# Strassen's seven products for y·w1 and y·w2, and an earlier hand-over of attention's memory

## The chip, the cores and the metric

The kernel runs on one core of a Trainium2 chip. The metric is the device time of one execution, in microseconds (us). Engines are named as in the profile: PE multiplies matrices, PEld loads its weights, DVE, ACT and POOL work on elements, SP issues the DMA transfers.

## The reference

Attention's output becomes the tokens of a first MLP, and its output those of a second, gated one. All of it is float64 on the host's side for the weights and float32 in the results:

```python
x = attention(q, k, v)                      # 4 x 576 tokens, 512 wide
h = x @ w_in; x = np.maximum(0.01*h, h) @ w_out     # 512 -> 2048 -> 512
a = x @ w1; b = x @ w2                      # 512 -> 1024 each
out = ((a * b) @ w3) @ w_out2               # 1024 -> 1024 -> 512
```

There are 2304 tokens. The kernel gets the weights as 64-bit words and converts them on the chip.

## The kernel before, in words

**Arithmetic.** Each float32 operand is kept as two parts, hi and lo; `split` makes hi with a copy (L107) and lo with a subtraction (L108). `mm3` (L112 to L114) then needs three matmuls for one product.

**Stages.** Attention (32 rounds) is interleaved with the first MLP. The MLP runs in 8 chunks of 320 or 256 tokens, with 16 turns f in each: `hidden(c, f)` is 12 matmuls into `ps_h`, `project(c, f)` 12 matmuls into `ps_x`, two turns later. Between them ACT makes `g`, and `gs` is split from it by DVE and POOL. A running number `turn` counts all turns, 16 to a chunk; at turn 80 chunk 5 begins, at 112 chunk 7.

**The fold.** w3·w_out2 is one 1024 x 512 matrix `wp`. Its 24 conversions (`conv3`: 8 pieces of w_out2, then 16 of w3) go through a class `Convert`: SP loads 512 KB of 64-bit words into one of two `rawf` buffers, POOL scales them into `wf` (L103), ACT makes two halves `rf` (L143, L145), DVE shifts and adds (L146, L147). The pieces of w_out2 are split and written to DRAM (`wo_dram` in the profile, tiles `wo2_` in the program's order). A piece of w3 is transposed by PE (`ps_w3T`, L546) and split into `w3T`. After nine conversions `wp_step` runs: 6 matmuls of 512 columns with a `wo2` tile read back from DRAM. The fold needs the memory that attention used, so it starts with chunk 5 (`C_LATE`).

**w1 and w2.** In chunk 7 their 16 pieces are converted (`raww`, `wr`) and stay in SBUF as `w12`.

**The gate and the final product.** For each of 6 chunks of 384 tokens and each of 8 column blocks i, `gate` runs 24 matmuls of 384 columns (`ps_ab`) for y·w1 and y·w2; ACT copies one half (`a`), DVE multiplies it by the other (`ab`), and `p` is split from that by ACT and POOL. `final` multiplies `p` by `wp` (`ps_y`, 512 columns, 24 matmuls for each of 18 blocks of 128 tokens).

The order of instructions on PE, DVE, ACT and POOL is set when the program is built, by a scheduler that reorders them within their dependences; each engine then runs its list strictly in order. SP's list is the queue of all DMA issues.

## Time and profile before

| | |
|---|---|
| median of 3 runs | 917.64 us (916.98 to 919.58) |
| the profiled execution | 918.02 us, span in the trace 916.2 us |
| PE busy | 880.8 us, 96% of the span |
| DVE, ACT, POOL busy | 345.9, 354.5, 247.8 us |
| DMA | 95.94 MB, mean 105 GB/s |

The span runs from the first instruction to the last; the execution is 1.8 us longer. PE's busy time counts overlapping matmuls once. In the trace of this kernel most matmuls of one L112-to-L114 group start evenly, so the distance between starts, not the mean duration, is the time that one takes.

### The profile page before, as it was taken

The page shows a single profiled execution, that of the slowest core. Times are in us where ns is not written, and L with a number is a line of the kernel's source. Part 1 is how long each engine was busy: PE and PEld are TensorE (multiplying, and loading weights), DVE is VectorE, ACT ScalarE, POOL GpSimd, SP SyncE. Part 2 cuts the span into 40 slices and gives each one's busy share as a digit, 9 for nine tenths or more (in the row PEclk, how much of TensorE's full clock was granted, in tenths as well). Part 3 has the DMA queues.
Part 4 walks back from the last instruction along what each step waited for, and adds up shares of the span by engine and source line. Part 5 has one row for each costly group of instructions (what it writes and reads, how often), then busy time and mean ns, then how long its engine had stood idle before and what let it go on. Part 6 is the DMA issues. An engine that isn't in the chain of part 4 may idle for free.

```text
span 916.2 us, 16026 instructions
## 1 busy us (share of the span) xinstructions
PE 880.8 (96%) x6456; PEld 832.4 (91%) x6456; DVE 345.9 (38%) x699; ACT 354.5 (39%) x904; POOL 247.8 (27%) x288
## 2 busy tenths in 40 slices
...
GB/s 170 313 271 129 180 19 57 83 48 73 49 44 78 45 14 62 47 252 282 235 293 271 211 201 160 202 79 1 46 24 35 35 35 24 12 24 12 12 24 35
DMA packets 110938, 95.94 MB, mean 105 GB/s; under 512 B 69520, under 2 KB 94352, under 8 KB 110864
## 3 DMA queue, kind: packets, MB, share of 16 engines
...
q8 instruction: 51, 0.84, 0.4%
...
## 4 chain that ended last, share of the span: by engine, by line
PE 82%; DVE 6%; ACT 3%; DMA 3%; SPq 2%; issue 2%; POOL 1%; DVEq 0%; POOLq 0%; ACTq 0%
PE ps_ab L112 7%; PE ps_ab L114 7%; PE ps_ab L113 7%; PE ps_h L113 6%; PE ps_h L114 6%; PE ps_x L112 6%; PE ps_h L112 6%; PE ps_x L114 6%; PE ps_x L113 6%; PE ps_y L113 4%; PE ps_y L112 4%; PE ps_y L114 4%; PE ps_s L328 2%; PE ps_o L389 2%; PE ps_wp L114 2%
## 5 line engine op out<-in xcount | busy, mean ns | idle before, releaser
L112 PE MATMUL ps_h<-x,win 128*128 128x320 f32 (+1 forms) x512 | 154.7, 303 | 3.6 <-DMA v<-in_v_dram 2.3
L113 PE MATMUL ps_h<-x,win 128*128 128x320 f32 (+1 forms) x512 | 155.4, 304 | 1.1 <-DVE x L422 1.1
L113 PE MATMUL ps_x<-gs,wout 128*128 128x320 f32 (+1 forms) x512 | 152.8, 299 | 2.4 <-DVE gs L108 2.4
L114 PE MATMUL ps_h<-x,win 128*128 128x320 f32 (+1 forms) x512 | 154.4, 302 | 0.0
L112 PE MATMUL ps_x<-gs,wout 128*128 128x320 f32 (+1 forms) x512 | 152.1, 299 | 1.1 <-DVE x L509 1.1
L114 PE MATMUL ps_x<-gs,wout 128*128 128x320 f32 (+1 forms) x512 | 152.7, 299 | 0.0
L112 PE MATMUL ps_ab<-ys,w 128*128 128x384 f32 x384 | 130.1, 339 | 0.0
L114 PE MATMUL ps_ab<-ys,w 128*128 128x384 f32 x384 | 130.0, 339 | 0.0
L113 PE MATMUL ps_ab<-ys,w 128*128 128x384 f32 x384 | 130.0, 338 | 0.0
L616 DVE TENSOR_TENSOR ab<-a,ps_ab 128x384 f32<-128x384 f32 x48 | 26.6, 554 | 253.0 <-ACT a L614 247.9
L107 DVE CAST gs<-g 128x320 fp32r<-128x320 f32 (+1 forms) x128 | 49.7, 391 | 153.6 <-ACT g L473 153.4
L108 POOL TENSOR_TENSOR p<-ab,p 128x384 fp32r<-128x384 f32 x48 | 48.5, 1011 | 218.6 <-ACT p L107 218.6
L108 POOL TENSOR_TENSOR gs<-g,gs 128x320 fp32r<-128x320 f32 (+1 forms) x80 | 66.4, 831 | 145.2 <-DVE gs L107 145.2
L112 PEld LDWEIGHTS ps_h<-x,win 128*128 128x128 f32 x512 | 97.9, 192 | 5.3 <-ACT x L420 4.2
L113 PEld LDWEIGHTS ps_x<-gs,wout 128*128 128x128 f32 x512 | 96.9, 189 | 3.8 <-DVE gs L108 2.9
L113 PEld LDWEIGHTS ps_h<-x,win 128*128 128x128 f32 x512 | 98.3, 192 | 2.1 <-DVE x L422 1.3
L112 PEld LDWEIGHTS ps_x<-gs,wout 128*128 128x128 f32 x512 | 96.5, 189 | 2.6 <-DVE x L509 1.3
L114 PEld LDWEIGHTS ps_h<-x,win 128*128 128x128 f32 x512 | 98.4, 192 | 0.3
L114 PEld LDWEIGHTS ps_x<-gs,wout 128*128 128x128 f32 x512 | 96.9, 189 | 0.5
L473 ACT ACTIVATE g<-ps_h 128x320 f32<-128x320 f32 (+1 forms) x128 | 51.4, 403 | 115.2 <-PE ps_h L114 114.1
L614 ACT COPY a<-ps_ab 128x384 f32<-128x384 f32 x48 | 23.0, 480 | 143.9 <-PE ps_ab L114 143.9
L112 PEld LDWEIGHTS ps_ab<-ys,w 128*128 128x128 f32 x384 | 72.0, 188 | 1.2
...
## 6 DMA issues: line engine op xcount, KB each, us to landing
...
```

Source lines behind the costliest of these rows:

```text
L107: copy_on(e_hi)(hi, src)
L108: e_lo.tensor_tensor(lo, src, hi.bitcast(F32), op=ALU.subtract)
L112: nc.tensor.matmul(ps, a[1], b[0], start=first, stop=False)
L113: nc.tensor.matmul(ps, a[0], b[1], start=False, stop=False)
L114: nc.tensor.matmul(ps, a[0], b[0], start=False, stop=last)
L328: nc.tensor.matmul(ps[j * QB : (j + 1) * QB, i - bl.start], qt[d, i * QB : (i + 1) * QB], kt[d, first_key(i, plain) : first_key(i, plain) ...
L389: nc.tensor.matmul(ps[j * D : (j + 1) * D, i * QB : (i + 1) * QB], vt[i][:, h + j, :], t[:, i, j * QB : (j + 1) * QB], start=True, stop=True,)
L473: nc.scalar.activation(g, ps, AF.Prelu, alpha=SLOPE)
L614: nc.scalar.copy(t, ps[0][:, :TB])
L616: nc.vector.tensor_tensor(g, t, ps[1][:, :TB], op=ALU.mult)
```

## The change

The second MLP's y·w1 and y·w2 are computed together as one 2 x 2 block product: tokens in two halves, the inner dimension in two halves, and [w1 w2] as two column blocks. Seven products (S1 to S7) take the place of eight, each 6 matmuls of 384 columns. A chunk now has 768 tokens, and there are 3 (`NCB`). The weight sums are made once, while converting (`keep_w12`, `wsum`), split and written to DRAM (`wq_dram`, 56 blocks of 256 KB); 28 tiles of two blocks are read back by `load_wq` into the 16 slots of the first MLP's `win`. Twelve of them stay; the other 16 are loaded for each chunk of tokens into slots that earlier tiles gave up. `split_y` makes seven sums of y, and `gate` recombines the seven PSUM results.

Attention's memory is given up at turn 72 (chunk 4, f = 8) in place of turn 80. The fold runs from there in 16 turns, one or two steps in a turn, and the conversion of w1 and w2 from turn 88 (chunk 5, f = 8) to the end of chunk 6. In chunk 7 the tiles of `wq` are loaded as the `win` slots come free. The final products of a chunk follow its gates.

```diff
-    NCB = T // TB
+    NCB = T // TB // 2
...
+    NS = 7
+    S1, S3, S4, S7, S6, S5, S2 = range(NS)
+    H2 = NC // 2
+    wq_dram = tc.dram_tile([P, NI * NS, 2 * H2 * P], F32, name="wq_dram")
+    yf, ys, pr, wq, w_f32 = {}, {}, {}, {}, {}
+
+    def keep_w12(m, i):
+        def finish(w, e_hi, e_lo):
+            w_f32[m] = w.rearrange("p (h c) -> p h c", h=2)
+            if m == 0:
+                return
+            a, b = w_f32.pop(0), w_f32.pop(1)
+            t, t_b = (
+                late.tile([P, n, 2, H2 * P], F32R, tag=f"wq{n}", name=f"wq{i}_{n}", bufs=m)
+                for n, m in ((S7, 1), (NS - S7, 1))
+            )
+            sums = (
+                (S1, a[:, 0], b[:, 1], ALU.add), (S7, a[:, 1], b[:, 1], ALU.subtract),
+                (S6, b[:, 0], a[:, 0], ALU.subtract), (S5, a[:, 0], a[:, 1], ALU.add),
+                (S2, b[:, 0], b[:, 1], ALU.add),
+            )
+            u = late.tile([P, len(sums), H2 * P], F32, tag="wsum", name=f"wsum{i}", bufs=1)
+            for j, (_, x, y, op) in enumerate(sums):
+                (nc.gpsimd if j % 2 else nc.vector).tensor_tensor(u[:, j], x, y, op=op)
+            split(t[:, S3, 0], t[:, S3, 1], a[:, 0], nc.scalar, nc.vector)
+            split(t[:, S4, 0], t[:, S4, 1], b[:, 1], nc.scalar, nc.vector)
+
+            split(t[:, S1, 0], t[:, S1, 1], u[:, 0], nc.scalar, nc.gpsimd)
+            nc.sync.dma_start(wq_dram[:, i * NS : i * NS + S7, :], t.bitcast(F32))
+            split(t_b[:, :, 0], t_b[:, :, 1], u[:, 1:], nc.scalar, nc.vector)
+            nc.sync.dma_start(wq_dram[:, i * NS + S7 : (i + 1) * NS, :], t_b.bitcast(F32))
+
+        return finish
+
+    def load_wq(j):
+
+        t = win_p.tile([P, 2, 2, H2, P], F32R, tag="win", name=f"wq{len(wq)}_{j}", bufs=NF)
+        nc.sync.dma_start(t.bitcast(F32), wq_dram[:, 2 * j : 2 * j + 2, :])
+        for x in range(2):
+            wq[divmod(2 * j + x, NS)] = t[:, x]
...
+    NWQ = NI * NS // 2
+    NWQ_STAY = 12
...
+        ops = {
+            S1: ((0, 0), (1, 1), ALU.add), S3: ((0, 1), (1, 1), ALU.subtract),
+            S4: ((1, 0), (0, 0), ALU.subtract), S7: ((1, 0), (1, 1), ALU.add),
+            S6: ((0, 0), (0, 1), ALU.add),
+        }
+        if m in ops:
+            (h0, x0), (h1, x1), op = ops[m]
+            u = yp.tile([P, TB], F32, tag="ysum", name=f"ysum{c}_{cc}_{m}", bufs=2)
+            (nc.gpsimd if m % 2 else nc.vector).tensor_tensor(u, t[:, h0, x0], t[:, h1, x1], op=op)
+        else:
+            u = t[:, 1, 1] if m == S5 else t[:, 0, 0]
+        split(y[:, 0, cc], y[:, 1, cc], u, nc.scalar, nc.vector if m % 2 else nc.gpsimd)
...
+        ps = {}
+
+        def product(m, out):
+            ps[m] = out
+            w, y = wq[i, m], ys[c, m]
+            for k in range(H2):
+                mm3(out, parts(w, k), parts(y, k), k == 0, k == H2 - 1)
+
+        def kept(m, nm):
+            t = fin.tile([P, TB], F32, tag=nm, name=f"{nm}{c}_{i}", bufs=2)
+            nc.scalar.copy(t, ps[m])
+            return t
+
+        both = [bank2(f"ps_ab{c}_{i}_{x}") for x in range(2)]
+        product(S1, both[0][:, 0, :TB])
+        product(S3, both[0][:, 1, :TB])
+        t1, t3 = kept(S1, "s1"), kept(S3, "s3")
+        product(S4, both[1][:, 0, :TB])
+        t4 = kept(S4, "s4")
+        product(S7, both[1][:, 1, :TB])
+        a1 = fin.tile([P, TB], F32, tag="a1", name=f"a1_{c}_{i}", bufs=2)
+        nc.vector.tensor_tensor(a1, t1, ps[S7], op=ALU.add)
+        nc.gpsimd.tensor_tensor(a1, a1, t4, op=ALU.add)
+        product(S6, side_bank(f"ps_ab{c}_{i}_6")[:, :TB])
+        nc.vector.tensor_tensor(t1, t1, ps[S6], op=ALU.add)
+        nc.gpsimd.tensor_tensor(t1, t1, t3, op=ALU.add)
+        product(S5, side_bank(f"ps_ab{c}_{i}_5")[:, :TB])
+        nc.vector.tensor_tensor(a1, a1, ps[S5], op=ALU.subtract)
+        nc.vector.tensor_tensor(t3, t3, ps[S5], op=ALU.add)
+        product(S2, bank(f"ps_ab{c}_{i}_2")[:, :TB])
+        nc.vector.tensor_tensor(t4, t4, ps[S2], op=ALU.add)
+        nc.vector.tensor_tensor(t1, t1, ps[S2], op=ALU.subtract)
+
+        for x, (a, b) in enumerate(((a1, t4), (t3, t1))):
+            nc.vector.tensor_tensor(a, a, b, op=ALU.mult)
+            gg = fin.tile([P, 2, TB], F32R, tag="p", name=f"p{c}_{x}_{i}", bufs=2 * NI)
+            split(gg[:, 0], gg[:, 1], a, nc.scalar, nc.gpsimd)
+            pr[2 * c + x, i] = gg
...
-        C_LATE = 5
+        T_FOLD, T_GATE = 72, 88
+        WQ_LAG = 3
...
+                conv.rest()
+                late_es.close()
+                xsA_es.close()
+                y_es, yp = pool("y", "right")
+                load_y(0, 0)
...
+                if turn == T_FOLD:
+                    step(*[stream] * 200)
+                    att_es.close()
...
+                if turn == T_GATE:
+                    while conv3.made < len(conv3.jobs) or conv3.done or w3T:
+                        fold_step()
+                    fold_es.close()
+                    late_es, late = pool("late", "right")
...
+                        jobs, late_tile("raw", U64, 2), late_tile("w", I32, 3), late_tile("r", I32, 2),
...
-                if c < C_LATE:
+                if turn < T_FOLD:
                     pace(c)
+                elif turn < T_GATE:
+                    fold_step()
+                    if f % 2:
+                        fold_step()
                 elif c < NCH - 1:
-                    fold_step()
+                    if f % 8 != 7:
+                        conv.step()
                 lagged()
                 if c == NCH - 1:
-                    conv.step()
-                    if 2 <= f < 2 + NI:
-                        load_wp(f - 2)
-                    if 3 <= f < 3 + NI:
-                        split_wp(f - 3)
-                    if 11 <= f < 11 + NC:
-                        split_y(0, f - 11)
-                    if f == 11 + NC - 1:
-                        load_y(1)
+                    if f >= WQ_LAG:
+                        load_wq(f - WQ_LAG)
+                    if f < H2 * NS:
+                        split_y(0, f // NS, f % NS)
+                    if f == NS - 1:
+                        load_y(0, 1)
+        for j in range(NF - WQ_LAG, NF):
+            load_wq(j)
         while todo:
             project(*todo.pop(0))
-        conv.step()
 
         xsB_es.close()
         wo2_es.close()
+        mlp_es.close()
         fin_es, fin = pool("fin", "left")
         for c in range(NCB):
+            if c > 0:
+                for j in range(NWQ_STAY, NF):
+                    load_wq(j)
             for i in range(NI):
                 gate(c, i)
-                if c > 0 and 1 <= i < 1 + TB // P:
-                    final(c - 1, i - 1)
-                if i >= NI - NC and c + 1 < NCB:
-                    split_y(c + 1, i - (NI - NC))
-            if c + 2 < NCB:
-                load_y(c + 2)
-        for tb in range(TB // P):
-            final(NCB - 1, tb, 2 if tb == TB // P - 1 else 1)
-        for es in (fin_es, late_es, mlp_es, wo_es, win_es, xsA_es):
+                if c == 0:
+                    load_wp(i)
+                    split_wp(i)
+                for j in range(NF, NWQ):
+                    if (2 * (j - NF + NWQ_STAY) + 1) // NS == i:
+                        load_wq(j)
```

PE's list around the place where the fold enters. `ps_h4_15` is turn 15 of chunk 4, `gs4_14` the projection's operand of turn 14, `ps_w3T0` the transposition of the first piece of w3 and `wf8` the ninth converted piece. Before:

```order
L112 MATMUL ps_h4_15_5042<-x2_0_3316,win15_1643 128x320 [waits Activation_49]
...
L112 MATMUL ps_x4_0_0_4637<-gs4_13_4997,wout13_1547 128x320 [waits DVE_49]
...
L112 MATMUL ps_h5_0_5080<-x2_0_3316,win0_657 128x256 [waits Activation_49]
...
L112 MATMUL ps_x4_0_0_4637<-gs4_14_5027,wout14_1633 128x320 [waits DVE_49]
...
L112 MATMUL ps_h5_9_5471<-x2_0_3316,win9_1230 128x256 [waits Activation_49]
...
L546 MATMUL ps_w3T0_5498<-ident_80,wf8_5446 128x128 [waits Activation_49]
L546 MATMUL ps_w3T0_5498<-ident_80,wf8_5446 128x128 x3
```

After:

```order
L112 MATMUL ps_h4_14_5134<-x2_0_3317,win14_1591 128x320 [waits Activation_49]
...
L112 MATMUL ps_x4_0_0_4638<-gs4_12_5050,wout12_1493 128x320 [waits DVE_49]
...
L112 MATMUL ps_x4_0_0_4638<-gs4_13_5093,wout13_1548 128x320 [waits DVE_49]
...
L112 MATMUL ps_x4_0_0_4638<-gs4_14_5149,wout14_1634 128x320 [waits DVE_49]
...
L114 MATMUL ps_x4_0_1_4639<-gs4_14_5149,wout14_1634 128x320
L546 MATMUL ps_w3T0_5161<-ident_80,wf8_5109 128x128 [waits DVE_49]
L546 MATMUL ps_w3T0_5161<-ident_80,wf8_5109 128x128 x3
L112 MATMUL ps_h4_15_5187<-x2_0_3317,win15_1644 128x320 [waits Activation_49]
...
L546 MATMUL ps_w3T1_5214<-ident_80,wf9_5152 128x128 [waits DVE_49]
L546 MATMUL ps_w3T1_5214<-ident_80,wf9_5152 128x128 x3
L112 MATMUL ps_wp0_0_5222<-wo2_0_0_5169,w3T0_5166 128x512 [waits DMAHW1_49]
```

The transposition stood behind ten hidden turns of chunk 5; now it stands ahead of `ps_h4_15` and of everything in chunk 5, and the second one, of `wf9`, follows that turn.

POOL's list at the same time of the program; `wf5` to `wf9` are the sixth to tenth piece. Before:

```order
L108 TENSOR_TENSOR gs4_14_5027<-g4_14_5025,gs4_14_5027 128x320 [waits DVE_49]
L108 TENSOR_TENSOR wo2_3_5283<-wf3_5231,wo2_3_5283 128x512 [waits Activation_49]
L103 TENSOR_SCALAR wf5_5317<-rawf5_5238 128x512 [waits DMAHW7_49,Pool_49]
L108 TENSOR_TENSOR gs4_15_5057<-g4_15_5055,gs4_15_5057 128x320 [waits DVE_49]
L108 TENSOR_TENSOR gs5_0_5095<-g5_0_5093,gs5_0_5095 128x256 [waits DVE_49]
L103 TENSOR_SCALAR wf6_5360<-rawf6_5281 128x512 [waits DMAHW1_49]
L108 TENSOR_TENSOR wo2_5_5369<-wf5_5317,wo2_5_5369 128x512 [waits DMAHW6_49,Activation_49]
L108 TENSOR_TENSOR gs5_1_5134<-g5_1_5132,gs5_1_5134 128x256 [waits DVE_49]
```

After:

```order
L108 TENSOR_TENSOR gs4_14_5149<-g4_14_5147,gs4_14_5149 128x320 [waits DVE_49]
L108 TENSOR_TENSOR wo2_3_5006<-wf3_4954,wo2_3_5006 128x512 [waits Activation_49]
L103 TENSOR_SCALAR wf5_5010<-rawf5_4961 128x512 [waits DMAHW7_49,Pool_49]
L108 TENSOR_TENSOR wo2_5_5062<-wf5_5010,wo2_5_5062 128x512 [waits DMAHW6_49,Activation_49]
L103 TENSOR_SCALAR wf6_5053<-rawf6_5004 128x512 [waits DMAHW1_49]
L103 TENSOR_SCALAR wf7_5096<-rawf7_5017 128x512 [waits DMAHW4_49,Pool_49]
L108 TENSOR_TENSOR wo2_7_5118<-wf7_5096,wo2_7_5118 128x512 [waits DMAHW2_49,Activation_49]
L103 TENSOR_SCALAR wf8_5109<-rawf8_5060 128x512 [waits DMAHW6_49]
L103 TENSOR_SCALAR wf9_5152<-rawf9_5103 128x512 [waits DMAHW0_49,Pool_49]
L108 TENSOR_TENSOR gs4_15_5202<-g4_15_5200,gs4_15_5202 128x320 [waits DVE_49]
```

Four operands `gs` stood among `wf5` to `wf9` and the split of pieces; now none stands between `wf5` and `wf9`. The rows ahead of this piece, from `wf0` on, stand in the same order in both.

DVE's list near the end of chunk 6 (`gs6_13` to `gs6_15`). `wl14`, `wl15` are pieces of w1 and w2, `wsum7` their sums and `wq7_` the split blocks. After:

```order
L146 TENSOR_SCALAR wl15_6792<-wl15_6792 128x512 [waits Pool_49]
L147 ISA wl15_6792<-wl15_6792,rl15_6793 128x1024 [waits DVE_49,Activation_49]
L107 CAST gs6_13_6934<-g6_13_6932 128x320 [waits Activation_49]
L108 TENSOR_TENSOR wq6_4_6745<-wsum6_6746,wq6_4_6745 128x4x256 [waits DMAHW7_49,Activation_49]
L596 TENSOR_TENSOR wsum7_6831<-wl14_6737,wl15_6792 128x256 [waits DVE_49]
L596 TENSOR_TENSOR wsum7_6831<-wl15_6792,wl14_6737 128x256
L596 TENSOR_TENSOR wsum7_6831<-wl15_6792 128x256
L108 TENSOR_TENSOR wq7_3_6829<-wl14_6737,wq7_3_6829 128x256 [waits DMAHW0_49,Activation_49]
L108 TENSOR_TENSOR wq7_3_6829<-wl15_6792,wq7_3_6829 128x256 [waits Activation_49]
L107 CAST gs6_14_6964<-g6_14_6962 128x320 [waits Activation_49]
L107 CAST gs6_15_6994<-g6_15_6992 128x320 [waits Activation_49]
L108 TENSOR_TENSOR wq7_4_6830<-wsum7_6831,wq7_4_6830 128x4x256 [waits DMAHW1_49,Activation_49]
```

Before, in chunk 6, `gs6_` stood among the fold's instructions:

```order
L107 CAST gs6_0_5927<-g6_0_5925 128x320 [waits Activation_49]
L108 TENSOR_TENSOR w3T7_5944<-ps_w3T7_5939,w3T7_5944 128x512 [waits Activation_49]
L146 TENSOR_SCALAR wf17_5993<-wf17_5993 128x512 [waits Pool_49]
L147 ISA wf17_5993<-wf17_5993,rf17_5994 128x1024 [waits DVE_49]
L107 CAST gs6_1_5990<-g6_1_5988 128x320 [waits Activation_49]
L108 TENSOR_TENSOR w3T8_6007<-ps_w3T8_6002,w3T8_6007 128x512 [waits Activation_49]
L146 TENSOR_SCALAR wf18_6068<-wf18_6068 128x512 [waits Pool_49]
L147 ISA wf18_6068<-wf18_6068,rf18_6069 128x1024 [waits DVE_49]
```

Three sums and three subtractions of a pair of pieces (the last of them of 1024 columns) stand on DVE where one conversion and a split out of PSUM stood; three more of each pair stand on POOL.

PE's list in the gate's second chunk, where weight tiles 15 to 18 (`wq56_15` to `wq56_18`) are used first; each wait on a DMA is for that tile:

```order
L112 MATMUL ps_ab1_4_1_8777<-ys1_2_8324,wq56_15_8490 128x384 [waits DMAHW5_49,Activation_49]
...
L112 MATMUL ps_ab1_4_6_8811<-ys1_4_8362,wq56_16_8772 128x384 [waits DMAHW0_49,DVE_49]
...
L112 MATMUL ps_ab1_4_1_8777<-ys1_3_8329,wq56_15_8490 128x384 [waits Activation_49]
...
L112 MATMUL ps_ab1_4_2_8829<-ys1_6_8370,wq56_17_8774 128x384 [waits DMAHW1_49]
...
L112 MATMUL ps_ab1_5_0_8852<-ys1_0_8286,wq56_17_8774 128x384
...
L112 MATMUL ps_ab1_5_0_8852<-ys1_1_8291,wq56_18_8846 128x384 [waits DMAHW2_49]
...
L112 MATMUL ps_ab1_5_1_8853<-ys1_2_8324,wq56_18_8846 128x384 [waits DVE_49]
```

Before, no `ps_ab` row waited on a DMA.

## Rows read from the trace of the kernel before

**Rows 1.** The page: the span, the engines' busy time with its share and the instructions, and the chain of work that ended last by engine.

```profile
span 916.2 us, 16026 instructions
...
PE 880.8 (96%) x6456; PEld 832.4 (91%) x6456; DVE 345.9 (38%) x699; ACT 354.5 (39%) x904; POOL 247.8 (27%) x288
...
PE 82%; DVE 6%; ACT 3%; DMA 3%; SPq 2%; issue 2%; POOL 1%; DVEq 0%; POOLq 0%; ACTq 0%
```

**Rows 2.** Stretches of the span: their ends and length, then busy time and count of PE, PEld, DVE, ACT, POOL, the granted PE clock, the DMA engines' busy share and GB/s.

```profile
400.00:420.00 20.00, 18.89 (x144) 18.34 (x143) 13.66 (x21) 11.87 (x22) 11.63 (x13) 1.00 0.92 317
440.00:470.00 30.00, 30.00 (x196) 27.30 (x195) 10.44 (x21) 11.81 (x24) 6.93 (x10) 1.00 0.84 282
470.00:500.00 30.00, 30.00 (x189) 27.83 (x188) 11.34 (x22) 10.79 (x21) 6.85 (x9) 1.00 0.85 287
560.00:600.00 40.00, 38.58 (x315) 38.17 (x314) 32.45 (x59) 28.42 (x52) 16.01 (x17) 1.00 0.60 182
609.00:760.00 151.00, 151.00 (x811) 144.03 (x810) 20.14 (x34) 35.79 (x73) 34.63 (x33) 1.00 0.09 30
```

**Rows 3.** PE in the gate, in order of time: start, duration. The lines left out are 25 more of the kind.

```profile
699.68 0.34 PE L114 MATMUL ps_ab<-ys,w 128*128 128x384 f32 x1
...
704.27 0.34 PE L113 MATMUL ps_ab<-ys,w 128*128 128x384 f32 x1
```

**Rows 4.** PE in the first fold turns, in order of time; in brackets the idle time before it and what ended it.

```profile
414.27 0.39 PE L112 MATMUL ps_x<-gs,wout 128*128 128x256 f32 x1 [1.11 <-DVE x L509]
```

**Rows 5.** POOL from the fold's first piece on: its first instruction on a piece of `rawf`, for the first two, the fifth, the ninth and the tenth.

```profile
389.43 1.26 POOL L103 TENSOR_SCALAR wf<-rawf 128x512 f32<-128x512 f32 x2
...
402.30 0.65 POOL L103 TENSOR_SCALAR wf<-rawf 128x512 f32<-128x512 f32 x1 [3.22 <-DMA rawf<-in_moe_w_out_dram]
...
416.98 0.65 POOL L103 TENSOR_SCALAR wf<-rawf 128x512 f32<-128x512 f32 x1 [1.63 <-DVE gs L107]
...
422.76 0.65 POOL L103 TENSOR_SCALAR wf<-rawf 128x512 f32<-128x512 f32 x1 [0.49 <-DMA rawf<-in_moe_w_dram]
```

**Rows 6.** PE where chunk 4 ends and the first turn of chunk 5 begins.

```profile
403.44 0.31 PE L113 MATMUL ps_x<-gs,wout 128*128 128x320 f32 x1
403.59 0.31 PE L114 MATMUL ps_x<-gs,wout 128*128 128x320 f32 x1
403.73 0.28 PE L112 MATMUL ps_h<-x,win 128*128 128x256 f32 x1
403.85 0.28 PE L113 MATMUL ps_h<-x,win 128*128 128x256 f32 x1
```

**Rows 7.** Groups of instructions from 388 to 600 us: shapes and count, busy time and mean ns, idle time before them and what ended it.

```profile
L108 POOL TENSOR_TENSOR gs<-g,gs 128x320 fp32r<-128x320 f32 x21 | 19.3, 917 | 38.1 <-DVE gs L107 38.1
L143 ACT ACTIVATE rf<-rawf 128x512 f16<-128x512 f32 x24 | 19.1, 794 | 49.5 <-DMA rawf<-in_moe_w_dram 46.8 <-DMA rawf<-in_moe_w_out_dram 2.7
L145 ACT ACTIVATE rf<-rawf 128x512 int16<-128x512 uint32 x24 | 18.4, 766 | 0.0
...
L108 POOL TENSOR_TENSOR gs<-g,gs 128x256 fp32r<-128x256 f32 x16 | 11.8, 746 | 16.5 <-DVE gs L107 16.5
...
L473 ACT ACTIVATE g<-ps_h 128x320 f32<-128x320 f32 x21 | 9.0, 430 | 27.9 <-PE ps_h L114 27.2 <-POOL wf L103 0.7
...
L107 ACT CAST wo<-wf 128x512 fp32r<-128x512 f32 x8 | 4.9, 614 | 4.8 <-DVE wf L147 4.8
```

**Rows 8.** SP's queue: issues of the fold's 512 KB pieces, with the time of issue.

```profile
434.93 4.60 SPq L521 DMA_DIRECT2D rawf<-in_moe_w_dram  x2
...
445.10 0.38 SPq L521 DMA_DIRECT2D rawf<-in_moe_w_dram  x1
...
456.26 0.38 SPq L521 DMA_DIRECT2D rawf<-in_moe_w_dram  x1
```

**Rows 9.** ACT's first instruction on such a piece, with ACT's wait for it.

```profile
438.74 0.79 ACT L143 ACTIVATE rf<-rawf 128x512 f16<-128x512 f32 x1 [4.12 <-DMA rawf<-in_moe_w_dram]
...
449.49 0.80 ACT L143 ACTIVATE rf<-rawf 128x512 f16<-128x512 f32 x1 [3.76 <-DMA rawf<-in_moe_w_dram]
...
461.75 0.80 ACT L143 ACTIVATE rf<-rawf 128x512 f16<-128x512 f32 x1 [2.86 <-DMA rawf<-in_moe_w_dram]
```

**Rows 10.** DVE late in chunk 7, in order of time.

```profile
588.39 0.29 DVE L107 CAST gs<-g 128x256 fp32r<-128x256 f32 x1
...
589.20 0.42 DVE L108 TENSOR_TENSOR gs<-g,gs 128x256 fp32r<-128x256 f32 x1
590.04 1.21 DVE L107 CAST gs<-g 128x256 fp32r<-128x256 f32 x1 [0.43 <-ACT g L473]
...
591.97 0.68 DVE L108 TENSOR_TENSOR w<-wr,w 128x512 fp32r<-128x512 f32 x1
...
593.97 0.41 DVE L146 TENSOR_SCALAR wr<-wr 128x512 int32<-128x512 int32 x1
594.52 0.69 DVE L147 CUSTOM_DVE_ANT_0 wr<-wr 128x1024 uint16<-128x1024 uint16 x1
```

**Rows 11.** POOL in the same stretch.

```profile
589.81 1.29 POOL L108 TENSOR_TENSOR wps<-wpf,wps 128x512 fp32r<-128x512 f32 x1 [2.66 <-ACT wps L107]
591.07 0.69 POOL L103 TENSOR_SCALAR wr<-raww 128x512 f32<-128x512 f32 x1
```

**Rows 12.** Groups of instructions from 609 us to the end, the gate's part.

```profile
L108 POOL TENSOR_TENSOR p<-ab,p 128x384 fp32r<-128x384 f32 x48 | 48.5, 1011 | 218.6 <-ACT p L107 218.6
...
L616 DVE TENSOR_TENSOR ab<-a,ps_ab 128x384 f32<-128x384 f32 x48 | 26.6, 554 | 253.0 <-ACT a L614 247.9 <-PE ps_ab L114 3.2 <-POOL p L108 1.9
L107 ACT CAST p<-ab 128x384 fp32r<-128x384 f32 x48 | 24.6, 513 | 31.9 <-DVE ab L616 31.9
L614 ACT COPY a<-ps_ab 128x384 f32<-128x384 f32 x48 | 23.0, 480 | 143.9 <-PE ps_ab L114 143.9
```

**Rows 13.** PE in the final product: two neighbouring matmuls of 512 columns.

```profile
623.13 0.40 PE L112 MATMUL ps_y<-wps,p 128*128 128x512 f32 x1
623.36 0.40 PE L113 MATMUL ps_y<-wps,p 128*128 128x512 f32 x1
```

More of the change, by code (lines that the diff above doesn't have):

```diff
@@ new lines, in load_wq, with load_y @@
+    def load_wq(j):
[5 more added lines that the diff above has]
+    NWQ_STAY = 12
+    def load_y(c, cc):
+        t = yp.tile([P, 2, 2 * TB], F32, tag="yf", name=f"yf{c}_{cc}", bufs=1)
+        for h in range(2):
+            r0 = (h * H2 + cc) * P
+            nc.sync.dma_start(t[:, h], x2_dram[r0 : r0 + P, c * 2 * TB : (c + 1) * 2 * TB])
+        yf[c, cc] = t.rearrange("p h (x t) -> p h x t", x=2)
```

101 lines of the change are left out of this document (36 added, 65 removed).

## The prediction

> **What bounds the kernel now.** I read the page first: PE is busy for 880.8 of 916.2 us and the chain that ended last lies on PE for 82% [rows 1]. Then the stretches: from 440 to 500 us and from 609 us to the end PE has no gap, at granted clock 1.00 [rows 2]. The two places behind attention where it does stop are small: a wait of 1.11 us for the copy of `ps_x` [rows 4], and between 560 and 600 us 40.00 less 38.58, that is 1.42 us [rows 2]. So time is won where PE has fewer matmuls, and lost wherever a moved piece of work makes PE wait; the other engines matter only through such waits.
>
> The unit of PE is the distance between starts: in the gate 26 steps from 699.68 to 704.27 us, 0.1765 us for 384 columns [rows 3]; in the first MLP 0.147 (320 columns) and 0.12 (256) [rows 6]; 0.23 for 512 [rows 13]. A turn half (12 matmuls) is thus 1.76 or 1.44 us.
>
> **What the change removes.** Before: 6 chunks x 8 blocks x 24 = 1152 gate matmuls. After: 3 x 8 x 7 x 6 = 1008. The 144 that go are worth 144 x 0.1765 = 25.4 us. The two old waits lie in code that moves away, so they go too: 2.5 us. All that PE keeps has the same shapes.
>
> **What it adds, in five places.**
>
> *The fold's entry.* The program's order puts the first transposition of w3 ahead of `ps_h4_15`, where PE arrived in before at 403.73 us [rows 6] (the work ahead of it is the same: one hidden half went behind it and one projection half ahead). It needs the ninth converted piece. Conversion of the first began at 389.43 us, straight behind attention's last piece, and stands at the same place in POOL's order, so I take the same start; POOL reached the ninth at 416.98 us and the tenth at 422.76 [rows 5]. In before PE had ten hidden turns to spare there. Bounds: at the old pace the wait is 416.98 + 0.55 - 403.73 = 13.8 us. From below by ACT alone: nine pieces of 0.794 + 0.766, eight splits of 0.614, three `g` of 0.430 [rows 7] make 20.2 us, the end at 408.7, a wait of 5.0. The old pace was set by transfers as well as engines: POOL waited 3.22 us for a piece [rows 5], and the DMA engines were 92% busy from 400 to 420 us [rows 2]. Some of what they carried there belongs to chunk 5, so they will be a little freer, and four `gs` are gone from among the pieces: I take 12.5. The tenth piece came 5.8 us behind the ninth, and only `ps_h4_15` (1.76 us) covers it: 0 to 4, I take 2. Together 14.5 us (5 to 18).
>
> *The rest of the fold.* It still has to move about 30 loads of `wo` and 14 pieces of 0.52 MB, and 2.1 MB of `wp`, 25 MB. PE's work there is 32 x 6 x 0.23 = 44 us of fold and 31 us of the MLP, 75 in all. That asks for 335 GB/s. The trace ran its 282 to 287 GB/s at a DMA share of 0.84 to 0.85, and 317 at 0.92 [rows 2]. At 317 it takes 79 us: 3 to 4 us of wait, I take 3; nothing at the least, since PE's wait at the entry lets loads run ahead, and 13 at 285 GB/s.
> The Trainium skill ("DMA: Bandwidth & Descriptors", Specifications) states about 358 GB/s as a core's limit to HBM. By it the 25 MB would need 70 us and this term would be nothing. No stretch quoted here ran that fast, so the sum keeps the row.
>
> *The conversion of w1 and w2.* It must end before chunk 7, and `gs6_14`, `gs6_15` queue behind it on DVE. In order its first piece stands behind `gs5_10`; from there PE has 75 us (13 halves of 256 columns, 32 of 320). DVE and POOL have: 16 conversions of 0.41 + 0.69 on DVE and 0.69 on POOL; for each of 8 pairs on DVE three sums and two subtractions of 256 columns at 0.42, and one of 1024, estimated from 0.42 (256) and 0.68 (512) as 1.2, so 3.3, and on POOL three at 0.746; 21 `gs` with 0.29 on DVE and 0.917 or 0.746 on POOL [rows 7, 10, 11]. That is 28.6 + 44.3 + 24.6 = 97.5 us on two engines. If they worked freely side by side, each would have about 49 us of 75, and nothing would be lost. The trace says they don't: a cast that takes 0.29 us took 1.21 when it met POOL's 1.29 us subtraction (590.04 against 589.81) [rows 10, 11]. And from 560 to 600 us they were busy for 32.45 + 16.01 = 48.5 us in 40 [rows 2], 1.21 per us with the waits for each other in it, and PE stopped. I take 1.15 per us: 84.8 us, 9.7 lost. Bounds: 0 (no hindrance), 22 (one at a time).
>
> *Weight tiles in the gate.* In chunks 0 and 1 of three, twelve loads each fill slots that PE has just given up. Counted in matmuls of 0.1765 us, the slot comes free 3.2 to 6.4 us ahead of need, for seven of them 4.2 or less. A piece of the same size landed 3.8 us after issue when alone (434.93 to 438.74), 4.4 and 5.5 with two loads beside it [rows 8, 9]. The gate's loads follow every 2.1 us, so some overlap: at 4.5 a chunk loses some 2.5 us, 5 in all. At 3.8 it is 1, at 5.5 17.
>
> *Hand-offs in the gate.* A block i now takes PE 42 x 0.1765 = 7.4 us. From it come 6 DVE operations out of PSUM (0.554 each) and two products, 3.3 + 1.4 us; on POOL two sums and two `p` of about 1.01 each, 4.0; on ACT three copies and two casts, 2.5 [rows 12]. None fills 7.4 us, but a PSUM bank comes free within about one product (1.06 us) of need, and the first gate follows fresh y sums and `wp` splits: 3 us (0 to 14).
>
> **The sum.** The profiled execution took 918.0 us, 0.4 above the median 917.6 and inside the runs shown (917.0 to 919.6). 918.0 - 25.4 - 2.5 + 14.5 + 3 + 9.7 + 5 + 3 = 925.3 us: slower by 0.8%.
>
> **Rivals.**
> 1. *The conversions keep their engines' own pace* (faster). Place: fold's entry and chunk 6. If nine pieces take ACT's 20.2 us (wait 5) and DVE and POOL don't hinder each other (0), the sum falls by 9.5 + 9.7 to 906. It decides from 10.4 us recovered (under 914.9). For it: outside the quoted collisions many casts took 0.29. Against it: the 3.22 us wait on a transfer and the 92% [rows 2, 5].
> 2. *Weight tiles come late* (slower). Landing at 5.5 us in the gate makes 17 of 5: 937. For it: 5.5 was seen with loads beside [rows 8, 9]. Against: the gate carried only 30 GB/s before [rows 2], 250 after.
> 3. *DVE and POOL exclude each other fully* in chunk 6: 97.5 - 75 = 22 lost, 938. For it: the 1.21 us cast [rows 10]. Against: 1.21 busy per us, though that counts waiting.
> The Trainium skill ("SBUF — State Buffer", Who interferes with whom) describes an exclusive lock on a port pair that these two share, taken by DVE operations with two SBUF inputs or in a two-port mode, and not by one out of PSUM. By that rule the collision of rows 10 and 11 is the normal case, and the added sums would all be of the locking kind.
> 4. *The waits overlap* (no change): what PE waits at the entry is used by the queues behind, so the rest of the fold costs nothing and chunk 6 only 5: about 917.
>
> **Chances.** Forecast 0.40 (919 to 932), rival 1 0.20, rival 2 0.15, rival 3 0.12, rival 4 0.13. Faster by over 0.3% (under 914.9) 0.20, within 0.3%, which is about what a measurement here can tell from no change, 0.13, slower 0.67. The range goes from rival 1's 906, raised to 908 to leave a tenth below, to 940 above rivals 2 and 3.
>
> **What would show it.** Gate: `ps_ab` 1008 times at 0.1765 us. Entry: PE waiting 10 to 14 us before the first `ps_w3T`, released by the ninth piece; if it waits under 6, rival 1 is on its way. Fold: PE waiting at `ps_wp` for DMA, some 3 us. Chunk 6: PE waiting at `ps_x` for `gs`, or at chunk 7's start, about 10 us, with DVE and POOL together busy over 1.1 per us. Gate: waits for `wq` of some 5 us in the first two chunks, none in the third. The prediction is wrong if the transposition's operand is ready by 406 us, or if the order's waits are met because the elementwise engines ran ahead of PE.

## The result and the profile after

The changed kernel takes 930.97 us (median of three, 928.81 to 930.98) where the kernel before takes 917.64: 1.0135 times as long, 95% interval 1.0111 to 1.0158. The forecast was 925.3, in a range of 908 to 940. The profiled execution took 930.97 us, its span is 929.2.

The page of the changed kernel: span, busy time, the chain by engine, and one of the three groups of gate matmuls.

```profile
span 929.2 us, 16361 instructions
...
PE 868.1 (93%) x6312; PEld 811.3 (87%) x6312; DVE 478.8 (52%) x899; ACT 381.4 (41%) x962; POOL 350.9 (38%) x384
...
PE 33%; DVE 8%; DMA 7%; POOL 4%; issue 3%; ACT 1%; SPq 0%; DVEq 0%; POOLq 0%; ACTq 0%
...
L112 PE MATMUL ps_ab<-ys,wq 128*128 128x384 f32 x336 | 114.4, 343 | 3.1 <-DMA wq<-wq_dram 1.7
```

Beside [rows 1], PE is busy for 12.7 us less (868.1 against 880.8) in a span that is 13.0 us longer, so it stands still for about 26 us more. Its 33% of the chain that ended last can't be set beside the 82% of [rows 1]: here the chain could be followed back only to 413 us, and the shares listed add up to 56% of the span. The gate has 3 x 336 = 1008 `ps_ab` matmuls, as predicted, at the spacing of [rows 3]: in the next fence 19 steps from 691.83 to 695.19 us, 0.177 us each.

PE inside a gate, in order of time (18 like them left out).

```profile
691.83 0.34 PE L113 MATMUL ps_ab<-ys,wq 128*128 128x384 f32 x1
...
695.19 0.34 PE L112 MATMUL ps_ab<-ys,wq 128*128 128x384 f32 x1
```

So the 25.4 us are won, and more than that is lost in waits. These are the longest of PE behind attention, from 388 us on (engine, its tile and line, what it waited for: us in total, times, longest).

```profile
PE ps_w3T L546 <- DVE wf L147: 14.7, 2, 13.9
PE ps_x L113 <- DVE gs L108: 3.3, 2, 2.3
PE ps_x L113 <- POOL gs L108: 3.1, 6, 1.1
PE ps_ab L112 <- DMA wq<-wq_dram: 1.7, 5, 0.6
PE ps_ab L112 <- DVE s L685: 1.3, 2, 0.7
```

And stretches of the changed kernel, columns as in [rows 2].

```profile
400.00:420.00 20.00, 5.92 (x36) 5.40 (x35) 10.13 (x16) 9.66 (x15) 7.84 (x9) 0.67 0.92 320
420.00:440.00 20.00, 19.39 (x100) 16.95 (x100) 9.11 (x16) 10.00 (x17) 4.84 (x7) 0.82 0.95 341
440.00:480.00 40.00, 39.16 (x250) 34.84 (x249) 18.47 (x33) 19.18 (x33) 8.99 (x13) 1.00 0.95 342
...
520.00:560.00 40.00, 37.57 (x255) 36.03 (x254) 34.33 (x54) 23.73 (x46) 28.04 (x32) 1.00 0.91 314
560.00:600.00 40.00, 38.69 (x277) 37.67 (x276) 29.46 (x44) 16.09 (x32) 22.61 (x23) 1.00 0.80 296
600.00:640.00 40.00, 35.55 (x274) 34.47 (x273) 29.59 (x37) 13.51 (x31) 23.65 (x19) 0.96 0.69 247
```

From 400 to 420 us PE worked 5.92 us; in [rows 2] it was 18.89. From 520 on it falls short in every stretch while DVE and POOL together are busy for more than the stretch lasts: 34.33 + 28.04 = 62.4 us of 40.

To size the waits I took the distances between starts of PE's matmuls and subtracted the median distance of their shape, which also counts the slow starts behind a wait. What remains: 19.3 us from 388 to 430, 1.6 in the rest of the fold, 5.9 in chunk 6, 7.8 in chunk 7, 8.0 in the gate and the final product. A chunk counts from its first hidden matmul, the gate from the first `ps_ab`. Together 42.6. Counted the same way the kernel before loses 5.6 us, and 42.6 - 5.6 - 25.4 = 11.6 of the 930.97 - 918.02 = 12.95 us by which the profiled executions differ. (By time, as the expectations below have it: 6.3 from 520 to 590 us, 7.4 from 610 to 640.)

### The profile page after: what moved, and what is told of

It is laid out like the page before. It is cut to its first block, busy times and chain, and to the rows that moved or that the text cites. A ratio compares the mean times of both kernels' runs of the same rounds, so it can differ in the third digit from the quotient of the medians.

```text
span 929.2 us, 16361 instructions
## 1 busy us (share of the span) xinstructions
PE 868.1 (93%) x6312; PEld 811.3 (87%) x6312; DVE 478.8 (52%) x899; ACT 381.4 (41%) x962; POOL 350.9 (38%) x384
## 4 chain that ended last, share of the span: by engine, by line
PE 33%; DVE 8%; DMA 7%; POOL 4%; issue 3%; ACT 1%; SPq 0%; DVEq 0%; POOLq 0%; ACTq 0%
PE ps_ab L112 5%; PE ps_ab L113 5%; PE ps_ab L114 5%; PE ps_y L112 3%; DMA yf<-x_dram 3%; PE ps_y L113 3%; PE ps_y L114 3%; DMA wq<-wq_dram 2%; PE ps_wp L112 2%; PE ps_wp L114 1%; PE ps_wp L113 1%; DVE ys L108 1%; DVE gs L107 1%; DVE ysum L638 1%; DMA wq_dram<-wq 1%
## 5 line engine op out<-in xcount | busy, mean ns | idle before, releaser
L108 POOL TENSOR_TENSOR gs<-g,gs 128x320 fp32r<-128x320 f32 (+1 forms) x80 | 74.0, 926 | 157.8 <-DVE gs L107 157.8
L112 PE MATMUL ps_ab<-ys,wq 128*128 128x384 f32 x336 | 114.4, 343 | 3.1 <-DMA wq<-wq_dram 1.7
L113 PE MATMUL ps_ab<-ys,wq 128*128 128x384 f32 x336 | 114.0, 339 | 1.1 <-POOL ys L108 1.1
L114 PE MATMUL ps_ab<-ys,wq 128*128 128x384 f32 x336 | 112.2, 338 | 0.0
L113 PEld LDWEIGHTS ps_x<-gs,wout 128*128 128x128 f32 x512 | 97.3, 190 | 11.5 <-POOL gs L108 5.5
L354 POOL TENSOR_TENSOR s<-s,rec 128x480 f32<-128x480 f32 (+1 forms) x32 | 31.0, 967 | 146.3 <-DVE rec L353 102.4
L112 PEld LDWEIGHTS ps_ab<-ys,wq 128*128 128x128 f32 x336 | 63.0, 188 | 7.3 <-DMA wq<-wq_dram 2.9
L667 ACT COPY s<-ps_ab 128x384 f32<-128x384 f32 x72 | 33.0, 482 | 88.6 <-PE ps_ab L114 82.5
L341 ACT ACTIVATE s<-s,nmax 128x96 f32<-128x96 f32 x144 | 52.1, 365 | 40.2 <-DVE nmax L338 39.9
```

Source lines behind the costliest of these rows:

```text
L108: e_lo.tensor_tensor(lo, src, hi.bitcast(F32), op=ALU.subtract)
L112: nc.tensor.matmul(ps, a[1], b[0], start=first, stop=False)
L113: nc.tensor.matmul(ps, a[0], b[1], start=False, stop=False)
L114: nc.tensor.matmul(ps, a[0], b[0], start=False, stop=last)
L341: nc.scalar.activation(s[:, i], s[:, i], AF.Exp, bias=nmax[:, i : i + 1], accum_out=total[:, i : i + 1])
L354: nc.gpsimd.tensor_tensor(s, s, rec[:, :nb].unsqueeze(2).to_broadcast([P, nb, KB]), op=ALU.mult)
```

## The experiments

Each is a small edit of the changed kernel, timed in three rounds beside the kernel before; ratios are to the kernel before, in brackets the 95% interval. The theories differ in whether a wait is pure loss or only takes the place of another, and, in chunk 6, in whether it is a single engine or DVE and POOL as a pair that is full.

**Is the entry's wait lost, or given back?** The fold's conversions start at turn 72 as in the changed kernel, but its PE steps only at turn 76, when the first pieces are ready; they end four turns later.

```diff
-        T_FOLD, T_GATE = 72, 88
+        T_FOLD, T_GATE = 72, 92
...
-                    fold_step()
-                    if f % 2:
+                    if turn >= 76:
+                        fold_step()
+                    if turn >= 84:
                         fold_step()
```

> Fold steps from turn 76 on, one in a turn to 83, two to 91; w1 and w2 from turn 92. The first transposition of w3 then stands behind four hidden turns of chunk 5. Theory A, the stall is given on: the wait at the entry (13.9 us) and the half-speed stretch behind it (about 4.5) go, but the fold's transfers and the conversion of w1 and w2 have the same work behind it and four turns less, so some 8 to 12 us come back there: 919 to 924 us. Theory B, the stall was idle time that nothing behind it needed: 911 to 914. Theory C, it only moves: 929 to 932.

Measured: 914.81 us, ratio 0.9959 (0.9945 to 0.9974); 16.2 us less than the changed kernel. Its stretches, columns as above:

```profile
400.00:420.00 20.00, 18.91 (x147) 18.68 (x146) 14.83 (x23) 12.36 (x23) 12.48 (x14) 1.00 0.93 317
420.00:440.00 20.00, 19.64 (x129) 17.50 (x128) 9.00 (x16) 9.17 (x15) 5.88 (x9) 1.00 1.00 369
440.00:480.00 40.00, 38.82 (x235) 33.88 (x234) 16.58 (x31) 19.36 (x33) 9.68 (x14) 1.00 0.96 349
...
520.00:560.00 40.00, 37.65 (x248) 36.14 (x247) 35.13 (x52) 23.06 (x42) 28.53 (x31) 1.00 0.90 305
```

PE is back at 18.91 us of 20 from 400 to 420. The stretch in which w1 and w2 are converted reads as it did (37.65 against 37.57 us from 520 to 560; 6.4 us lost from 520 to 590, against 6.3), though PE is 16 us further in its list there and chunk 7 begins at 567.3 us in place of 583.7. So the entry's wait was idle time, and taking it away did not lengthen that stretch. Elsewhere some came back: the rest of the fold loses 4.1 us in place of 1.6, and the gate 13.9 in place of 8.0, with PE's waits for `wq` at 5.7 us against 1.7; chunk 7 loses 2.1 in place of 7.8. The time lies 0.8 us above theory B's range and well below theory A's. The fold now runs at 349 to 369 GB/s.

**Is it the work ahead of PE, or the pieces?** 80 more matmuls of 256 columns fill PE's wait; they write the bank that the first transposition then overwrites, so nothing is left out. In the order that the scheduler made of it, `ps_h4_15` and one projection half (12 matmuls each) also moved ahead of the first transposition.

```diff
             ps = bank(f"ps_w3T{i}")
+            if i == 0:
+                for _ in range(80):
+                    nc.tensor.matmul(
+                        ps[:, :256], win[15][:, 0, 0], win[14][:, 0, :2].rearrange("p c f -> p (c f)"),
+                        start=True, stop=True,
+                    )
```

> Leaves nothing out, adds 80 matmuls of 256 columns (9.6 us at full clock) into the first transposition's bank, before the wait at the fold's entry; they are overwritten. Theory A, the clock: PE's idle 13.9 us is what brought the granted clock to 0.50 and kept it there until 427 us; with PE filled the wait shrinks to about 4 us, the clock stays at 1.00 and the work behind it runs at full speed, so about 4 us are won: 926 to 928. Theory B, the half speed comes from something else, or PE's work behind the wait would have waited anyway: 930 to 932, with the clock low again or the waits moved to the fold's products.

Measured: 932.52 us, ratio 1.0153 (1.0136 to 1.0170): no gain. (The profiled execution took 936.0 us, the longest of four.) PE there, in order of time, with the idle time before each and what ended it:

```profile
419.49 0.66 PE L552 MATMUL ps_w3T<-ident,wf 128*128 128x128 f32 x4 [1.43 <-DVE wf L147]
423.55 1.11 PE L552 MATMUL ps_w3T<-ident,wf 128*128 128x128 f32 x4 [3.40 <-DVE wf L147]
424.32 0.78 PE L112 MATMUL ps_wp<-wo,w3T 128*128 128x512 f32 x1
```

The same place in the changed kernel:

```profile
404.31 0.31 PE L114 MATMUL ps_x<-gs,wout 128*128 128x320 f32 x1
418.51 1.11 PE L546 MATMUL ps_w3T<-ident,wf 128*128 128x128 f32 x4 [13.89 <-DVE wf L147]
419.27 0.61 PE L112 MATMUL ps_h<-x,win 128*128 128x320 f32 x1
...
423.43 1.11 PE L546 MATMUL ps_w3T<-ident,wf 128*128 128x128 f32 x4 [0.61 <-DVE w3T L108]
424.20 0.78 PE L112 MATMUL ps_wp<-wo,w3T 128*128 128x512 f32 x1
424.77 0.63 PE L113 MATMUL ps_wp<-wo,w3T 128*128 128x512 f32 x1
...
427.33 0.42 PE L113 MATMUL ps_wp<-wo,w3T 128*128 128x512 f32 x1
```

The first `ps_wp` product starts at 424.32 us, in the changed kernel at 424.20. With PE kept busy the wait only moves: 1.43 us to the first transposition, 3.40 to the second. The tenth piece sets the entry's end. In the filled kernel the second transposition waits for that piece itself; in the changed kernel it waits for the split of the first transposition, which follows the tenth piece on DVE without a pause:

```profile
422.08 0.69 DVE L147 CUSTOM_DVE_ANT_0 wf<-wf,rf 128x1024 uint16<-128x1024 uint16 x1 [0.27 <-ACT rf L145]
422.69 0.68 DVE L108 TENSOR_TENSOR w3T<-ps_w3T,w3T 128x512 fp32r<-128x512 f32 x1
```

Neither of the two waits for PE, so the half clock up to there cost nothing that the traces show. The clock after the wait is a separate, small loss: from 424.77 to 427.33 us the products start 0.43 us apart where they take 0.23 [rows 13]. Filling did not avoid it: the granted clock from 420 to 430 us is 0.83 in that run, behind the 3.40 us gap that remains.

**Is chunk 6 bound by DVE and POOL as a pair?** The first step of converting w1 and w2, 16 scalings of about 0.65 us, goes from POOL to ACT, which is not in the pair.

```diff
-    LAST_CONV = ("GAD",)
+    LAST_CONV = ("AAD",)
```

> The first scaling of each piece of w1 and w2 moves from POOL (0.65 us each, 16 times) to ACT. Theory A, DVE and POOL shut each other out while converting: with 11 us of 97 gone from the pair, the waits of 520 to 600 us (6.3 us) fall to 2 or less: 925 to 928. Theory B, the transfers set the pace there, or ACT is late next: 930 to 933.

Measured: 923.72 us, ratio 1.0061 (1.0046 to 1.0076), somewhat below theory A's range. And the same step put on DVE, which stays in the pair but is the busier of the two:

```diff
-    LAST_CONV = ("GAD",)
+    LAST_CONV = ("DAD",)
```

> As e3, but the scaling of the pieces of w1 and w2 goes from POOL to DVE: POOL has 10 to 11 us less, DVE some 7 to 11 more. Theory A, what counts from 520 to 600 us is the sum on the pair, which shut each other out: at most 4 of 97 us less, the waits stay near 6 us, 928 to 932. Theory B, POOL's list alone is late there (the operands gs queue behind its conversions): relieved as in e3, 922 to 926.

Measured: 924.40 us, ratio 1.0067 (1.0050 to 1.0084): in theory B's range, 3.6 us below theory A's. The stretch from 520 to 560 us, first with the step on ACT, then on DVE:

```profile
520.00:560.00 40.00, 39.49 (x274) 39.23 (x273) 37.07 (x61) 29.46 (x56) 23.37 (x25) 1.00 0.95 330
```

```profile
520.00:560.00 40.00, 38.32 (x267) 37.92 (x267) 39.32 (x63) 25.22 (x49) 24.40 (x24) 1.00 0.92 315
```

PE works 39.49 us of 40 in the first and 38.32 in the second, against 37.57; chunk 6 loses 0.7 and 3.5 us, against 5.9. The two times are nearly the same for another reason: most of the second kernel's gain lies in chunk 7 (3.2 us lost, against 7.8; 5.9 with the step on ACT), where its data for y came earlier (DVE waits 0.57 and 1.32 us for `yf`, in the changed kernel 2.83, 3.35 and 4.45). So the times do not tell the theories apart, and chunk 6 does. Were POOL's list alone late, both edits would have relieved it alike. Loading DVE more (39.32 of 40) made it better, not worse, so DVE alone is not what is full. Out of the pair nearly all is won; inside it a part, for DVE does the step in 0.41 us at best and POOL in 0.64. That speaks for the pair.

How the two hinder each other is seen in the changed kernel's durations: operations on `wsum` and from it, from 500 to 600 us (ns minimum/median/maximum).

```profile
L596 DVE TENSOR_TENSOR wsum<-wl,wl x16: 411/955/1100, 514.8 to 581.3; 128x256 f32<-128x256 f32 x16
...
L596 POOL TENSOR_TENSOR wsum<-wl x8: 728/919/927, 510.1 to 581.9; 128x256 f32<-128x256 f32 x8
...
L108 POOL TENSOR_TENSOR wq<-wsum,wq x8: 749/917/927, 516.3 to 582.8; 128x256 fp32r<-128x256 f32 x8
L108 DVE TENSOR_TENSOR wq<-wsum,wq x8: 1210/1212/1256, 518.5 to 585.4; 128x1024 fp32r<-128x1024 f32 x8
```

256 columns take DVE 0.41 us at best and 0.96 in the median; POOL's go from 0.73 to 0.92. The gate tells which operations suffer. Two kinds of DVE's operations there, of 384 columns each:

```profile
L684 DVE TENSOR_TENSOR a<-a,ps_ab x24: 542/554/555, 653.8 to 894.6; 128x384 f32<-128x384 f32 x24
L691 DVE TENSOR_TENSOR s<-s,s x24: 548/550/1374, 656.2 to 896.9; 128x384 f32<-128x384 f32 x24
```

The first reads `ps_ab`, in PSUM; all 24 ran while POOL worked, and none took over 0.56 us. The second reads SBUF alone and took up to 1.37. Of all DVE's operations of 384 columns from 600 us on, 85 with an operand in PSUM overlapped with one of POOL and took 0.54 to 0.56 us. Of those with all operands in SBUF, 42 had no such overlap and took 0.54 to 0.56, and 41 had one and took 0.55 to 1.65, 1.26 in the median. What the two shut each other out of is work on SBUF.

If every instruction counts by the short end of its kind's durations (the tenth percentile), DVE and POOL got through 1.25, 1.18 and 1.23 us of work per us in the three stretches of 20 us from 520 to 580; 1.24 and 1.20 with the step on ACT (520 to 560), 1.28, 1.25 and 1.29 in the three with it on DVE. Neighbours on an engine overlap by some 0.08 us; less that, it is 1.13, 1.08 and 1.11 in the changed kernel. The pair does little more than one engine's work.

**Does chunk 7 wait for y's data?** By the rows of DVE there, the casts of `gs` stand in its list behind a sum that waits for `yf`:

```profile
610.18 0.43 DVE L108 TENSOR_TENSOR gs<-g,gs 128x256 fp32r<-128x256 f32 x1
613.96 0.56 DVE L638 TENSOR_TENSOR ysum<-yf 128x384 f32<-128x384 f32 x1 [3.35 <-DMA yf<-x_dram]
614.44 1.10 DVE L107 CAST gs<-g 128x256 fp32r<-128x256 f32 x1
...
616.74 1.48 DVE L108 TENSOR_TENSOR gs<-g,gs 128x256 fp32r<-128x256 f32 x1
```

PE then waits for `gs`: at 615.60 us for 0.43 us, at 618.27 for 2.29. The next load of `yf` was issued at 608.38 us, when its one buffer came free. Two buffers, and both halves loaded together (one buffer less of `wpf` makes room):

```diff
-        t = yp.tile([P, 2, 2 * TB], F32, tag="yf", name=f"yf{c}_{cc}", bufs=1)
+        t = yp.tile([P, 2, 2 * TB], F32, tag="yf", name=f"yf{c}_{cc}", bufs=2)
...
-        t = yp.tile([P, DM], F32, tag="wpf", name=f"wpf{ib}", bufs=2)
+        t = yp.tile([P, DM], F32, tag="wpf", name=f"wpf{ib}", bufs=1)
...
                 load_y(c + 1, 0)
+                load_y(c + 1, 1)
```

> Two buffers for yf (and one for wpf), both halves of y loaded together. Theory A: in chunk 7 DVE's list stands still for 3.4 and 4.5 us behind sums that wait for a half of y, with the operands gs of the MLP behind them, and that is the 7.3 us that PE loses from 610 to 640 us; with the data there early 4 to 6 of these go: 925 to 927. Theory B, DVE and POOL simply have too much there: 929 to 932.

Measured: 935.70 us, ratio 1.0190 (1.0175 to 1.0205), slower still and above both ranges. Chunk 7 loses 4.6 us in place of 7.8, but the gate 16.2 in place of 8.0: the first gate now waits for the banks that ACT has to empty, for 1.50 and 1.15 us,

```profile
644.88 0.45 PE L112 MATMUL ps_ab<-ys,wq 128*128 128x384 f32 x1 [1.50 <-ACT s L667]
```

and at the ends of the first two gate chunks PE waits 1.88 and 3.29 us for DVE. So the waits for y are part of chunk 7's loss, but the edit brought waits of its own that cost more. As a test of what they are worth it is inconclusive.

**Do the weight tiles cost their waits?** With 8 tiles staying in place of 12, the slots are free earlier.

```diff
-    NWQ_STAY = 12
+    NWQ_STAY = 8
```

> Eight weight tiles stay in the gate in place of twelve, so eight slots rotate and a load has at least 6 us, mostly 9 to 15, instead of 3 to 6; eight more loads of 512 KB in all. Theory A, the tiles' landing is what PE waits for in the gate's first chunks: their 2.7 us of waits go and nothing new comes, 927 to 929 us. Theory B, the waits at a tile hide others (a PSUM bank, a y sum) that come right behind: 930 to 932.

Measured: 930.79 us, ratio 1.0141 (1.0105 to 1.0177): no change that can be told, in executions from 927.31 to 934.45.

```profile
640.00:700.00 60.00, 60.00 (x342) 59.48 (x341) 31.35 (x58) 19.81 (x42) 29.90 (x30) 1.00 0.52 168
700.00:720.00 20.00, 17.29 (x65) 13.51 (x64) 14.22 (x19) 7.49 (x15) 13.74 (x13) 0.83 0.34 116
```

From 640 to 700 us PE has no gap left, and no wait for `wq` appears; but from 700 to 720, where the first chunk of the gate ends, it works 17.29 of 20 us, at a granted clock of 0.83, behind the recombination on DVE (L685) and the new `ys`. These waits took the others' place.

**Is the early hand-over worth it?** Memory given up at turn 80 as in the kernel before, w1 and w2 converted from turn 96, a step in every turn.

```diff
-        T_FOLD, T_GATE = 72, 88
+        T_FOLD, T_GATE = 80, 96
...
-                    if f % 8 != 7:
-                        conv.step()
+                    conv.step()
```

> Strassen's products kept, attention's memory given up at turn 80 as in the kernel before; the fold to turn 95, w1 and w2 from 96 to the end of chunk 6, one piece in each turn. Theory A, the hand-over at turn 72 is what costs at the entry (no PE wait for the first transposition here), but the conversion of w1 and w2 with its 97 us of DVE and POOL work has only 57 us of PE beside it, so 20 us or more are lost at chunk 6's end: 925 to 940. Theory B, the conversion runs ahead of PE far enough: 908 to 916.

Measured: 923.30 us, ratio 1.0068 (1.0045 to 1.0090), between the two ranges. No wait at the entry; but the gate begins at 615.6 us (639.6 in the changed kernel), while y is split only from 610 us on (597 there), behind the conversion. From 620 to 640 us PE worked 14.61 us of 20, mostly waiting for parts of y:

```profile
620.00:640.00 20.00, 14.61 (x46) 11.61 (x45) 10.59 (x8) 8.99 (x20) 15.50 (x13) 0.66 0.44 132
```

```profile
PE ps_ab L112 <- ACT ys L107: 4.2, 3, 1.9
```

(The second line counts from 615 to 640 us.) Chunks 6 and 7 lose 7.7 us, less than the 13.7 of the changed kernel, and the gate 27.1, against 8.0. The kernel that hands over at 72 and takes the fold's steps on PE from turn 76 is 8.5 us faster (923.30 less 914.81); with the steps at once it is slower. The two also differ in where the conversion of w1 and w2 begins (turn 96 and 92) and in its pace, so the 8.5 us are not the hand-over's alone.

**Do the gains add up?** The first and the third edit together, and then with 8 tiles staying as well; no line is new.

> The edits of e1 and e3 together. Theory A, the two losses are separate (the fold's entry, and DVE with POOL in chunk 6): about 16 and 7 us add up, 906 to 910 us. Theory B, once the entry is cured chunk 6 sits so close behind the fold that ACT, or the transfers, set its pace: the second edit brings under 3 us, 912 to 915.

> The edits of e1, e3 and e6 together. If the three losses are separate, 903 to 908 us; if they hide each other, 909 to 914.

Measured: 906.74 us, ratio 0.9881 (0.9865 to 0.9898), and 906.33 us, ratio 0.9869 (0.9853 to 0.9885). The single gains, 16.2 and 7.3 us, make 23.5; measured are 24.2. The tiles add nothing that can be told. The last one's page:

```profile
span 904.4 us, 16377 instructions
...
PE 860.2 (95%) x6312; PEld 807.4 (89%) x6312; DVE 470.1 (52%) x899; ACT 389.5 (43%) x978; POOL 335.2 (37%) x368
```

Both are faster than the kernel before by more than 1%, and both lie in the range in which the losses are separate.

**Where each kernel loses.** The profiled executions, in us by spacing of starts. The gate's column holds the final product too.

| kernel | 388 to 430 us | to chunk 6 | chunk 6 | chunk 7 | gate | sum |
|---|---|---|---|---|---|---|
| before | 1.7 | 0.2 | 0.3 | 1.9 | 1.5 | 5.6 |
| changed | 19.3 | 1.6 | 5.9 | 7.8 | 8.0 | 42.6 |
| fold's steps from turn 76 | 1.6 | 4.1 | 5.1 | 2.1 | 13.9 | 26.8 |
| wait filled | 9.5 | 3.0 | 5.5 | 8.0 | 12.4 | 38.3 |
| scaling on ACT | 19.5 | 1.3 | 0.7 | 5.9 | 9.5 | 36.9 |
| scaling on DVE | 19.4 | 1.4 | 3.5 | 3.2 | 9.8 | 37.4 |
| two buffers for y | 18.6 | 1.6 | 6.1 | 4.6 | 16.2 | 47.0 |
| 8 tiles stay | 19.4 | 1.3 | 6.1 | 7.8 | 11.5 | 46.1 |
| hand-over at turn 80 | 2.3 | 0.6 | 4.0 | 3.7 | 27.1 | 37.7 |
| turn 76 and ACT | 2.3 | 3.7 | 0.8 | 0.6 | 12.2 | 19.6 |
| and 8 tiles | 2.3 | 4.9 | 0.2 | 0.5 | 11.5 | 19.4 |

The filler's own 9.6 us are not in its row. In every experiment the gate loses more than the changed kernel's 8.0 us, so part of what is gained ahead comes back there; in the fastest two the gate holds well over half of what is left.

## Why the prediction was right in sign and 5.7 us short

*What is removed* (25.4 and 2.5 us) stands: 144 matmuls fewer at the same spacing. Of the two old waits the one at chunk 5's start is gone (it is back, with 1.09 us, where the fold's steps begin at turn 76); the one for `gs` late in chunk 7 gave way to longer ones, counted there.

*The fold's entry* (14.5) is the term that was mis-sized most among those of the sum: 19.3. POOL's pieces show its parts.

```profile
416.39 0.65 POOL L103 TENSOR_SCALAR wf<-rawf 128x512 f32<-128x512 f32 x1
420.69 0.66 POOL L103 TENSOR_SCALAR wf<-rawf 128x512 f32<-128x512 f32 x1 [3.66 <-DMA rawf<-in_moe_w_dram]
```

The ninth piece came at 416.39 us, 0.6 earlier than in [rows 5]; I had taken 1.3. What it needs behind POOL was also too small: the sum has 0.55 us from POOL's start to the transposition, which is less than POOL's own 0.65 and leaves out the halves on ACT and the shift and the sum on DVE; it took 418.51 - 416.39 = 2.12. As PE came 0.9 later than I took, at 404.62 us, it waited 13.89 us in place of 12.5 (14.2 by spacing of starts). "The tenth piece came 5.8 us behind the ninth ... I take 2": here it came 4.3 behind, POOL waited 3.66 us for its transfer, and from 418.51 us to the first product at 424.20 PE lost 3.2 us, its low clock within that. The clock I had left out altogether: 0.58 from 424 to 428 us, which cost 1.3 us more. 14.2 + 3.2 + 1.3 is 18.7; the rest lies ahead of the wait.

*The rest of the fold* (3) was 1.6. The wait that I expected, at `ps_wp` for a transfer, did not come; the one wait there is 0.84 us, at 447.03 us, of a transposition for its piece. That the entry's wait lets the fold run ahead, the reason given for the lower end, fits: without that wait the fold loses 4.1. The transfers were not held at 317 GB/s: 341 and 342 in the changed kernel, 369 and 349 when the fold's steps started later. The sentence on the Trainium skill's page "DMA: Bandwidth & Descriptors" (Specifications, about 358 GB/s) was nearer than the row that the sum kept, yet as a limit it is passed: 369 GB/s over 20 us, and 417 from 404 to 408 us.

*The conversion of w1 and w2* (9.7) cost 5.9 in chunk 6. The mechanism holds, and the size was off by the pace: in the same measure as the sum's 97.5 us (undisturbed durations) the two engines got through about 1.22 us per us, not 1.15, and 97.5 / 1.22 is 80 us beside PE's 75. My 1.21 busy per us from [rows 2] was no measure of that, though it lies near: it held waits for each other, and here such a sum reaches 1.56. The rule of the Trainium skill ("SBUF — State Buffer", Who interferes with whom), that operations like these exclude each other and those out of PSUM do not, is what the trace shows (1.26 us in the median against 0.54 to 0.56). Rival 3 had the mechanism too, but its 22 us took full durations as exclusive.

*Chunk 7* (7.8) is the loss for which the sum had no number of its own, and the largest thing that it left out. The text looked for the conversion's loss at `ps_x` "or at chunk 7's start", but priced only the time up to there; y's sums, which wait for their data with casts of `gs` behind them, were counted under the hand-offs. How the 7.8 us split into late data and a full pair is open: the kernels that relieved the pair lost 5.9 and 3.2 there, the one with two buffers 4.6.

*Weight tiles* (5) and *hand-offs* (3) were 8.0 together, as forecast, but not as split: PE's waits for `wq` sum to only 1.7 us. Taking those away won nothing, since the waits at the ends of the gate's chunks grew.

That the sum came within 5.7 us is in part luck: entry and chunk 7 cost 12.6 us more than it held, the rest of the fold and the conversion 5.2 less.

*The rivals.* The conversions did not keep their own pace (rival 1): the entry's pieces came at the old one. Tiles did not come late (rival 2). That waits overlap (rival 4) is refuted for entry and chunk 6 by the run in which the one went and the other stayed (5.1 us, against 5.9). It holds for entry and rest of the fold (1.6 with the entry's wait, 4.1 without), for tiles and hand-offs, and in part between chunk 7 and the gate.
